# Attention, then a low-rank mixer, on one core: the low-rank sum laid out by transfers, mixing of one tile ahead of scores, conversions in other steps

## The chip, the cores and the metric

The kernel runs on one core of a Trainium2 chip. The metric is the device time of one launch in microseconds (us), as a median of several runs. One more execution was taken by the hardware profiler; all lines shown below come from it.

## The reference

Inputs are q, k, v of shape (4, 8, 768, 64) and eight decay factors lam in float32, and four weights U, V, w_ch1, w_ch2 in float64. Only what matters is shown:

```python
def _attn_ref(q, k, v, lam):            # block = 64
    for b in range(nb):
        intra = (qb @ kb^T) * Dmask          # lam ** (i - j), lower triangle
        intra = intra @ vb
        inter = (qb * lam_pow) @ kv_state
        out[:, :, sl] = intra + inter
        kv_state = lam_block * kv_state + (kb * rev_pow)^T @ vb

def _moe_ref(x, U, V, w_ch1, w_ch2):    # x: (4, 768, 512), all heads side by side
    xt = x.transpose(0, 2, 1)
    h = xt @ U @ V                       # U: 768 x 32, V: 32 x 768, over the sequence
    u = x + h.transpose(0, 2, 1)
    ch = np.maximum(u @ w_ch1, 0.0) @ w_ch2   # 512 x 2048 and 2048 x 512
    return u + ch
```

So each of the four batches needs all of its 768 rows of x before the low-rank sum (x^T U, 512 x 32) is known; then every row tile gets its share of V added (the "mixing"), and the result u goes into two large products.

## The kernel before

**Stages.** The rows of the four batches are cut into 24 tiles of 128 rows, six in a batch. Step s computes the attention of tile s and, on the side, finishes tile `done` = s - 7 of the batch before (mixing, transposing, splitting into parts for the product). After step 23 comes the first large product in "units": a unit (`hidden`) is one slice of 128 of the 2048 hidden columns for a pair of 512-row groups, with 24 matmuls of 128x512; into the first units the leftovers of the last batch are put (`rest`, L893 and on). Then comes the second product. The order of instructions on every engine is written out by hand in the list `pieces` (L653 to L685) and, for the first units, in `rest`, `at` and `side`: every engine runs its own instructions in that order and waits where an operand isn't there.

**One step (L659 to L685).** For tile s: `fade` (ScalarE, L401, from the third tile of a batch), `mix` and `turn` of earlier tiles (TensorE, L567 and L630), `split` (ScalarE L644, VectorE L645), `prep` of tile s+1 (transposes of q and k on TensorE, L361; copies out by ScalarE, L367; then the load of a later q tile), `scale` (GpSimd, L392 for q and L381 for k), `mixed` (VectorE, L579), `intra` and `state` (L455, L427), the next v load on ScalarE's queue, `inter` (L466, then ScalarE's copy of x, L472), `scores` of tile s+1 (L408), `low` at the end of a batch (L482), `aside` (a piece of weight conversion), `masked` of tile s+1 (VectorE, L417), then `store` of a finished tile and the next k load on SyncE's queue. At s = 0, 4, 5 and 6 `aside` comes after `masked`.

**The low-rank sum.** `low(b)` (L477) makes x^T U of batch b in one PSUM tile `pp` of 128 x 128: four groups of 32 partitions, one for each quarter of the 512 columns. It shares its PSUM slot (tag "px") with the output of `intra`. The mixing reads `p_hl`, four groups of 32 partitions by 512 columns: in each half of the partitions (two groups) the high part of 256 columns in the left half, the low part in the right half. Each quarter is needed on two groups of partitions, its own and a neighbour's. ScalarE copies two quarters of `pp` side by side into `p_f` (L492), VectorE the other two (L524) and then masks off the high bits into `p_h` (L527). In the next step three pieces follow by `next_of_low`: four ScalarE copies place the high part (L535), GpSimd subtracts twice for the low part (L539), two ScalarE copies place the low part on the other two groups (L546). The last batch goes another way (L499 to L520), which is not touched.

**The mixing.** `mix(s)` is four matmuls of 64 x 128 by 64 x 256 into the right half of the PSUM tile `pm` (one buffer); the transposes of the tile before (`turn(s - 1)`) write the left half of the same buffer. `mixed(s)` adds the result to x.

**Conversions.** The weights come as float64 words and are made into float32 by steps: fetches on SyncE's queue (L146), `one` (VectorE L166 and, unless `apart`, `mantissa` L155; ScalarE L173 and L174), `two` (L184), `three` (L192), `four` (L197), and for w_ch1 the split `five` (ScalarE L215), `six` (L220), `seven` (L227). `aside(s)` issues them; the ScalarE parts are held back to `late`. The numbers in L744 to L747 say in which step each is put; what is left at NS (24) goes into the first units (L907). The words go in turn into the buffers of `words_pool` (L139).

Of the kernel before, what the change touches and what calls it, by code (L numbers as in the profile page):

```python
# [8 lines left out]
FP32 = mybir.dt.float32  # L9
# [9 lines left out]
def kernel(  # L19
# [91 lines left out]
    def weight_steps(dst, src, n, rows=P, in_parts=False, apart=False):  # L111
# [23 lines left out]
        def fetch_part(i):  # L135
            if i == 0 and plain:
                st["loads"] = list(pieces(dst()))
            elif i == 0:
                words_pool.append(words_pool.pop(0))  # L139
                words = words_pool[-1].tile([P, 2 * C], U32, tag="words", name="words")  # L140
                words = words[0:rows, 0 : 2 * n]
                st["loads"] = list(pieces(words))
                st["w"] = words.rearrange("p (n two) -> p n two", two=2)
# [331 lines left out]
    pps, others = {}, {}  # L475

    def low(b):  # L477
# [12 lines left out]
        pps[b] = rows_f = tmp("p_f")[0:R]  # L490
        for g in range(2):
            nc.scalar.copy(rows_f[:, g * P : (g + 1) * P], pp[g * R : (g + 1) * R])  # L492
        others[b] = pp

    def low_rows(b):

        pp, t = pps.pop(b), tmp("p_h")[0:R]
        own = [(slice(g * R, (g + 1) * R), slice(g * P, (g + 1) * P)) for g in range(G)]
        if b == B - 1:  # L499
            h, h2, l, l2 = (p_hl[g * R : (g + 1) * R] for g in range(G))  # L500
# [21 lines left out]
        rows_f, pp = pp, others.pop(b)  # L522
        for g in range(2, G):
            nc.vector.tensor_copy(  # L524
                out=rows_f[:, g * P : (g + 1) * P], in_=pp[g * R : (g + 1) * R]
            )
        nc.vector.tensor_scalar(t.bitcast(U32), rows_f.bitcast(U32), HI, None, ALU.bitwise_and)  # L527
        wide = [slice(x * 2 * P, (x + 1) * 2 * P) for x in range(2)]

        def place(g, low):  # L530
            return p_hl[g * R : (g + 1) * R, wide[low]]

        def spread():
            for g in range(G):
                nc.scalar.copy(place(g, 0), t[:, wide[g // 2]])  # L535

        def low_part():
            for x in range(2):
                nc.gpsimd.tensor_tensor(  # L539
                    out=place(2 * x, 1), in0=rows_f[:, wide[x]], in1=t[:, wide[x]],  # L540
                    op=ALU.subtract,
                )

        def spread_low():
            for x in range(2):
                nc.scalar.copy(place(2 * x + 1, 1), place(2 * x, 1).bitcast(FP32))  # L546

        pps[b] = [spread, low_part, spread_low]
# [105 lines left out]
    for s in range(NS):  # L654
# [7 lines left out]
        step += [("mix", done)] * mixes + [("turn", done - 1)] * turns  # L662
# [3 lines left out]
        step += [("next_of_low", b - 1)] * rows + [("next_of_low", b - 1)] * rows  # L666
        step += [("scale", s + 1)] * more
        step += [("mixed", done)] * mixes
# [404 lines left out]
```

## Time and profile before

| | us |
|---|---|
| median of 3 runs | 653.47 (651.42 to 654.1) |
| profiled execution, its own time | 651.42 |
| its span, first to last instruction | 649.6 |
| steps of batch 0, to the scores of tile 6 | 0 to 31.18 |
| steps of batches 1, 2, 3 (to the scores of tile 12, of tile 18, to the first unit) | 31.18 to 58.27 to 86.99 to 115.36 |
| first four units with leftovers | 115.36 to 145.0 |
| the rest of both products | 145.0 to 649.6 |

TensorE's busy time in these five stretches is 28.62 of 31.18, 26.56 of 27.09, 27.29 of 28.72, 27.40 of 28.37, and 29.25 of 29.64 us; from 145 to 640 us it is 494.97 of 495. The granted clock is 1.000 throughout. Because matmuls are pipelined and their ends are modelled, a short stall can hide in TensorE's busy time; the distance from one step's scores to the next step's scores shows it better. In undisturbed steps (42.44 to 55.37 us) that distance is 4.31 to 4.32 us.

### The profile page before, as it was taken

The numbers are of one execution on the slowest core, as the hardware profiler recorded it, in microseconds if no ns is written. First come the engines' busy times: TensorE is split into PE (matmuls) and PEld (weight loads), VectorE is DVE, ScalarE is ACT, GpSimd is POOL, SyncE is SP. The second block draws the span as 40 slices with busy tenths as digits, with TensorE's granted clock in tenths as the row PEclk, the third lists the DMA queues.
The fourth block names the chain that finished last, engine by engine and source line by source line (L and its number), as shares of the span: only waits on it lengthen the run. The fifth ranks groups of instructions, "written<-read, shape, count | busy, mean of one in ns | idle before, by whom it ended". The sixth has DMA issues, their size and how long they took to land.

```text
span 649.6 us, 13396 instructions
## 1 busy us (share of the span) xinstructions
PE 639.9 (99%) x5242; PEld 538.1 (83%) x5242; DVE 441.2 (68%) x722; ACT 273.1 (42%) x506; POOL 116.4 (18%) x98
## 2 busy tenths in 40 slices
PE   8999999999999999999999999999999999999997
PEld 7889889788888888888888888888888888888886
DVE  6776879658997777777796254685575665755854
ACT  4676767435664444444454221332322322322320
POOL 4466868240000000000000000030030300300300
PEclk9999999999999999999999999999999999999999
DMA  9989994265876656566687999864363363453521
GB/s 229 247 200 251 231 252 124 77 216 167 290 256 227 211 210 211 210 211 211 210 292 267 321 324 399 285 216 147 97 227 98 115 211 97 160 164 98 178 82 65
DMA packets 131776, 131.29 MB, mean 202 GB/s; under 512 B 81346, under 2 KB 89794, under 8 KB 131714
## 3 DMA queue, kind: packets, MB, share of 16 engines
q1 hardware_dynamic: 106592, 124.02, 59.8%
q10 hardware_dynamic: 25122, 6.42, 4.4%
q8 instruction: 41, 0.67, 0.5%
q14 instruction: 21, 0.17, 0.1%
HBM read 80.09 MB, written 50.33 MB: 201 GB/s over the span
## 4 chain that ended last, share of the span: by engine, by line
PE 94%; ACT 2%; DVE 1%; DMA 1%; issue 1%; DVEq 0%; ACTq 0%
PE pz L837 26%; PE pz L971 13%; PE pz L969 13%; PE pd L973 13%; PE pd L848 13%; PE pss L408 3%; PE px L455 3%; PE px L466 2%; PE pqk L361 1%; PE pkv L427 1%; DMA qraw<-in_q_dram 1%; PE pp L482 1%; PE pm L567 1%; PE pm L630 1%; PE put L608 1%
## 5 line engine op out<-in xcount | busy, mean ns | idle before, releaser
L837 PE MATMUL pz<-u_hl,w 128*128 128x512 f32 x768 | 184.5, 390 | 0.0
L837 PEld LDWEIGHTS pz<-u_hl,w 128*128 128x128 f32 x768 | 143.6, 188 | 30.1 <-ACT r L844 0.3
L971 PE MATMUL pz<-w_hl,m 128*128 128x512 f32 x384 | 148.6, 389 | 0.0
L969 PE MATMUL pz<-w_hl,m 128*128 128x512 f32 x384 | 148.2, 389 | 0.0
L973 PE MATMUL pd<-w_d,m 128*128 128x512 f32 x384 | 147.4, 389 | 0.0
L952 ACT ACTIVATE m<-rm 128x512 fp32r<-128x512 f32 x96 | 60.6, 632 | 183.5 <-PE pd L973 123.0
L953 DVE SCALAR_TENSOR_TENSOR m<-rm,m 128x512 fp32r<-128x512 f32 x96 | 71.5, 747 | 96.0 <-ACT m L952 95.9
L998 POOL TENSOR_TENSOR o<-o,u 128x512 f32<-128x512 f32 x20 | 29.8, 1522 | 433.4 <-DVE o L994 433.4
L853 DVE SCALAR_TENSOR_TENSOR r<-pd,r 128x512 f32<-128x512 f32 x96 | 61.7, 685 | 60.1 <-ACT r L844 48.0
L848 PE MATMUL pd<-u_d,w 128*128 128x512 f32 x384 | 95.9, 390 | 0.0
L973 PEld LDWEIGHTS pd<-w_d,m 128*128 128x128 f32 x384 | 72.1, 188 | 15.3 <-DVE m L954 0.5
L971 PEld LDWEIGHTS pz<-w_hl,m 128*128 128x128 f32 x384 | 72.1, 188 | 15.0
L969 PEld LDWEIGHTS pz<-w_hl,m 128*128 128x128 f32 x384 | 72.1, 188 | 14.9
L848 PEld LDWEIGHTS pd<-u_d,w 128*128 128x128 f32 x384 | 71.8, 188 | 14.8
L844 ACT ACTIVATE r<-pz 128x512 f32<-128x512 f32 x96 | 51.8, 590 | 64.8 <-PE pz L837 64.8
L954 DVE SCALAR_TENSOR_TENSOR m<-m 128x512 fp32r<-128x512 f32 x96 | 74.7, 780 | 3.0
L417 DVE TENSOR_TENSOR sm<-pss,mask 128x512 f32<-128x512 f32 x48 | 30.9, 684 | 15.4 <-PE pss L408 15.2
L215 ACT ACTIVATE w<-wf 128x512 fp32r<-128x512 f32 x32 | 20.3, 634 | 35.7 <-DVE wf L197 27.4
L173 ACT ACTIVATE sc<-sc,ends 128x512 f32<-128x512 uint32 x30 | 21.6, 721 | 23.2 <-DVE sc L166 23.1
L455 PE MATMUL px<-vraw,sm 128*64 128x64 f32 x768 | 28.4, 225 | 2.7 <-ACT u_hl L644 0.9
L455 PEld LDWEIGHTS px<-vraw,sm 128*64 128x64 f32 x768 | 25.2, 137 | 4.7 <-issue 1.3
L408 PE MATMUL pss<-qt,kt 64*128 64x128 f32 x384 | 28.8, 290 | 0.1
(92 smaller groups left out, 619.4 us busy)
## 6 DMA issues: line engine op xcount, KB each, us to landing
r_d<-r SPq DMA_DIRECT2D x96, 256.0 KB, 2.6
rm<-r_d SPq DMA_DIRECT2D x96, 256.0 KB, 2.7
words<-in_moe_w_ch_dram SPq DMA_DIRECT2D x30, 512.0 KB, 4.4
w_d<-w SPq DMA_DIRECT2D x16, 768.0 KB, 3.4
w_hl<-w_d SPq DMA_DIRECT2D x16, 512.0 KB, 6.1
u_d<-x_nat SPq DMA_DIRECT2D x24, 256.0 KB, 4.0
u<-u_d SPq DMA_DIRECT2D x24, 256.0 KB, 4.2
qraw<-in_q_dram SPq DMA_DIRECT2D x23, 256.0 KB, 4.1
```

Of the source, the lines that this page charges most:

```text
L408: nc.tensor.matmul(out=pss[:, x, a, :], lhsT=kt[half[x], a, :], rhs=qt[half[x], a, :], start=True, stop=True,)
L455: nc.tensor.matmul(out=px[half[t], x, a, :], lhsT=sm[:, x, a, half[t]], rhs=vr[:, 2 * a + x, :], start=(a == 0), stop=(alone and a == HP - 1),
L837: nc.tensor.matmul(out=like(acc[g][0], g), lhsT=w[:, n, ct, :], rhs=columns(uhl[g][:, n], g, ct), start=(ct == 0 and n == 0), stop=(ct == ...
L844: nc.scalar.mul(rs[g], acc[g][0], 4096.0 + 1.0)
L848: nc.tensor.matmul(out=like(acc[g][1], g), lhsT=w[:, 2, ct, :], rhs=columns(ud[g], g, ct), start=(ct == 0), stop=(ct == CT - 1),)
L853: nc.vector.scalar_tensor_tensor(rs[g], acc[g][1], 4096.0, rs[g], ALU.mult, ALU.add)
L952: nc.scalar.activation(out=m[:, 0], in_=r, func=AF.Relu, scale=NEAR)
L953: nc.vector.scalar_tensor_tensor(m[:, 1], r, 0.0, hi, ALU.max, ALU.subtract)
L954: nc.vector.scalar_tensor_tensor(m[:, 2], hi, E, low, ALU.mult, ALU.subtract)
L969: nc.tensor.matmul(out=pz, lhsT=m[:, 0, cols], rhs=hl[:, 0], start=first, stop=False)
L971: nc.tensor.matmul(out=pz, lhsT=m[:, 1, cols], rhs=hl[:, 1], start=False, stop=end)
L973: nc.tensor.matmul(out=pd, lhsT=m[:, 2, cols], rhs=dd, start=first, stop=end)
```

## The change

Five things are altered. (1) For batches 0 to 2 the low-rank sum is copied out of PSUM by one ScalarE copy of 128 x 128; in the next step four ScalarE copies of 32 x 128 round it into its own places, four GpSimd subtractions of 32 x 128 make the low part, and four SBUF-to-SBUF transfers of 32 x 2 x 128 on SyncE's queue lay both parts into the neighbour's places. The VectorE work and the mask are gone. (2) For the second tile of a batch's steps (c == 1, where the first tile of the batch before is mixed) `mix` and `mixed` come just ahead of the next scores, after `inter`. (3) The conversions of w_ch1's first two slices sit in other steps; the second slice's `three`, `four`, `five`, `six` move to the end of unit 0 and `seven` to the end of unit 1. (4) U's fetch moves from before step 0 to step 1 and its conversion from steps 1 and 2 to steps 2 and 3; V's fetches move from step 0 to step 2. (5) `words_pool` is turned the other way round, so that the buffers are used in another order.

```diff
-                words_pool.append(words_pool.pop(0))
-                words = words_pool[-1].tile([P, 2 * C], U32, tag="words", name="words")
+                words_pool.insert(0, words_pool.pop())
+                words = words_pool[0].tile([P, 2 * C], U32, tag="words", name="words")
...
     def low(b):
...
-        pps[b] = rows_f = tmp("p_f")[0:R]
-        for g in range(2):
-            nc.scalar.copy(rows_f[:, g * P : (g + 1) * P], pp[g * R : (g + 1) * R])
-        others[b] = pp
+        pps[b] = tmp("p_f")[:, 0:P]
+        nc.scalar.copy(pps[b], pp)
...
     def low_rows(b):
...
-        rows_f, pp = pp, others.pop(b)
-        for g in range(2, G):
-            nc.vector.tensor_copy(
-                out=rows_f[:, g * P : (g + 1) * P], in_=pp[g * R : (g + 1) * R]
-            )
-        nc.vector.tensor_scalar(t.bitcast(U32), rows_f.bitcast(U32), HI, None, ALU.bitwise_and)
-        wide = [slice(x * 2 * P, (x + 1) * 2 * P) for x in range(2)]
-        def place(g, low):
-            return p_hl[g * R : (g + 1) * R, wide[low]]
-        def spread():
-            for g in range(G):
-                nc.scalar.copy(place(g, 0), t[:, wide[g // 2]])
-        def low_part():
-            for x in range(2):
-                nc.gpsimd.tensor_tensor(
-                    out=place(2 * x, 1), in0=rows_f[:, wide[x]], in1=t[:, wide[x]],
-                    op=ALU.subtract,
-                )
-        def spread_low():
-            for x in range(2):
-                nc.scalar.copy(place(2 * x + 1, 1), place(2 * x, 1).bitcast(FP32))
-        pps[b] = [spread, low_part, spread_low]
+        def place(g, of, low):
+            return p_hl[g * R : (g + 1) * R, low * 2 * P + (of % 2) * P :][:, 0:P]
+        def own():
+            for g in range(G):
+                rows, at = pp[g * R : (g + 1) * R], place(g, g, 0)
+                nc.scalar.copy(at, rows)
+                nc.gpsimd.tensor_tensor(
+                    out=place(g, g, 1), in0=rows, in1=at.bitcast(FP32), op=ALU.subtract
+                )
+        def other():
+            for g in range(G):
+                at, of = (
+                    p_hl[x * R : (x + 1) * R].rearrange("r (l h c) -> r l h c", l=2, h=2)
+                    for x in (g ^ 1, g)
+                )
+                nc.sync.dma_start(
+                    out=at[:, :, g % 2].bitcast(FP32), in_=of[:, :, g % 2].bitcast(FP32)
+                )
+        pps[b] = [own, other]
...
-        step += [("mix", done)] * mixes + [("turn", done - 1)] * turns
+        step += [("mix", done)] * (mixes and c != 1) + [("turn", done - 1)] * turns
...
-        step += [("next_of_low", b - 1)] * rows + [("next_of_low", b - 1)] * rows
+        step += [("next_of_low", b - 1)] * rows
         step += [("scale", s + 1)] * more
-        step += [("mixed", done)] * mixes
+        step += [("mixed", done)] * (mixes and c != 1)
...
-        step += [("next_of_low", b - 1)] * rows
         both = [("intra", s), ("state", s)]
         step += (both if s > NT else both[::-1]) + [("next_v", s), ("inter", s)]
+        step += [("next_of_low", b - 1)] * rows
...
+        step += [("mix", done), ("mixed", done)] * (mixes and c == 1)
         step += [("scores", s + 1)] * more
...
-        (u_side, (-1, 1, 1, 2, 2)),
-        (v_steps(), (0, 0, 3, 3, 4, 4, 4, 5, 5)),
-        (w1_steps(0, True), (8, 9, 10, 11, 13, 14, 15, 16, 16, 17, 19)),
-        (w1_steps(1, True, True), (15, 16, 17, 18, 20, 20, 21, 22, 23, 23, NS, NS)),
+        (u_side, (1, 2, 2, 3, 3)),
+        (v_steps(), (2, 2, 3, 3, 4, 4, 4, 5, 5)),
+        (w1_steps(0, True, True), (8, 9, 10, 11, 12, 14, 15, 16, 17, 17, 20, 21)),
+        (w1_steps(1, True, True), (15, 16, 17, 18, 18, 22, 23, NS, NS, NS, NS, NS)),
...
-    aside(-1)
...
-    side = list(zip((0, 0), last)) + list(zip((0, 3, 3, 3, 4, 4, 4, 4), w1_steps(2)))
+    side = list(zip((0, 0, 0, 0, 1), last)) + list(zip((0, 3, 3, 3, 4, 4, 4, 4), w1_steps(2)))
```

## The prediction

> **What bounds the kernel now.** First the page's head: TensorE is busy nearly all the time, and the chain that ended last is almost all TensorE.
>
> ```profile
> PE 639.9 (99%) x5242; PEld 538.1 (83%) x5242; DVE 441.2 (68%) x722; ACT 273.1 (42%) x506; POOL 116.4 (18%) x98
> ...
> PE 94%; ACT 2%; DVE 1%; DMA 1%; issue 1%; DVEq 0%; ACTq 0%
> ```
>
> The change takes no matmul away, so it can only win back stalls or add some. The stretch from 145 to 640 us has TensorE busy for 494.97 of 495: nothing to win there, and what moves there (the words buffers' new order) costs nothing while TensorE's inputs are ready as now; if a fetch there came late, one unit would wait. All that counts lies ahead of 145 us. There I read TensorE's timeline from one step's scores (L408) to the next; a full undisturbed step takes 4.31. These lines show the stalls:
>
> ```profile
> 11.95 0.47 PE L361 MATMUL pqk<-ident,qraw 64*128 64x64 f32 x8 [0.40 <-DMA qraw<-in_q_dram]
> 16.37 0.47 PE L361 MATMUL pqk<-ident,qraw 64*128 64x64 f32 x8 [0.44 <-DMA qraw<-in_q_dram]
> ...
> 64.20 1.16 PE L408 MATMUL pss<-qt,kt 64*128 64x128 f32 x16
> ...
> 69.25 1.16 PE L408 MATMUL pss<-qt,kt 64*128 64x128 f32 x16
> ...
> 72.26 1.24 PE L455 MATMUL px<-vraw,sm 128*64 128x64 f32 x32 [0.87 <-ACT qt L367]
> ...
> 125.80 0.66 PE L608 MATMUL put<-ident,x_nat 128*128 128x128 f32 x4 [0.39 <-DVE x_nat L575]
> ```
>
> The reader sees three kinds: q tiles late in batch 0; steps of 5.05 instead of 4.31 where a batch's first tile is mixed (64.20 to 69.25), and the step after it (5.33, to 74.58); and a wait for VectorE in the first units. Summed over the three batch changes the steps are about 6 us longer than the undisturbed ones (5.27, 5.05, 5.33, 5.31, 4.96 against 4.31, and some 1.6 in the three steps before): that bounds the gain.
>
> Third, VectorE's and ScalarE's timelines, by which each part is costed:
>
> ```profile
> 14.74 1.11 DVE L155 TENSOR_SCALAR m<-words 128x192 uint32<-128x192 uint32 x1
> ...
> 16.16 1.28 DVE L417 TENSOR_TENSOR sm<-pss,mask 128x512 f32<-128x512 f32 x2
> ...
> 20.66 1.28 DVE L417 TENSOR_TENSOR sm<-pss,mask 128x512 f32<-128x512 f32 x2
> ...
> 70.05 1.51 DVE L155 TENSOR_SCALAR m<-words 128x512 uint32<-128x512 uint32 x1
> ```
> ```profile
> 63.10 1.66 ACT L535 CAST vp<-p_h 32x256 fp32r<-32x256 f32 x4
> ...
> 64.78 0.83 ACT L546 CAST vp<-vp 32x256 fp32r<-32x256 f32 x2
> ...
> 67.36 0.59 ACT L367 COPY kt<-pqk 128x512 f32<-128x512 f32 x1
> ```
>
> Conversion pieces stand ahead of `masked` (L417) on VectorE, and the placing copies ahead of the k copy (L367) that TensorE's `state` waits for.
>
> **U's and V's words: +1.1 us.** SyncE issued U at 7.99, ahead of two q tiles that then came 0.40 and 0.44 late. Moved behind k3, q3, k4, q4 and q5, U frees q3 (the first late tile, q2, is ahead of it and stays late). But `one` of U now stands ahead of step 2's `masked`. When does U land? SyncE's issues from 8.9 on take 1.69, 1.84, 1.69 and again some 1.6, so U is issued at about 15.9 and lands 4.5 later (U's own landing before), 20.4; by bytes it is a little earlier, since V's 192 KB no longer go ahead of it: 19.6. I take 20.0. Then L166, L155, L184: 2.05 as measured from 14.11 to 16.16, or about 1.1 if each takes the 0.36 that L184 took there. `masked` starts at 21.1 to 22.1 instead of 20.66, TensorE's `intra` 0.81 later (20.66 to 21.50 before, rounded), at 21.9 to 22.9 against 21.50: +0.4 to +1.4, +0.8 taken. In step 3 `three` and `four` of U (1.53 at 19.13 to 20.66) now join V's 2.2 ahead of `masked`: TensorE has 3.8 of work until it needs that result, VectorE needs 2.0 (masked, kv) + 2.2 to 3.7, so 0 to 1.4 more, 0.3 taken, since GpSimd is idle then. Bounds for the whole 0 to +3.0: below nothing if U comes by 18.5.
>
> VectorE's L155 took 1.11 for 192 columns while GpSimd's L381 ran (14.66 to 15.73), yet 0.48 on average for 512 columns later, mostly beside an idle GpSimd. The Trainium skill ("SBUF — State Buffer", SBUF: two separate sides) calls this a lock: the one that starts second is blocked for the other's whole instruction. By it U's three pieces cost 1.1 where no GpSimd instruction is under way at 20 us (the next, L392, comes near 21), and the sum would be 0.4 lower than with the middle value.
>
> **Copied out once, laid by transfers, mixing later.** I work out batch 2 (steps 12 to 14). ScalarE: two copies of 0.26 become one, but u_hl waits for TensorE until 61.6 anyway: nothing. VectorE loses two copies and a mask (0.59 + 0.42): they weren't last there. Four copies of 128 columns cost about 0.30 each (0.403 at 256 columns, 0.618 at 512), 1.2 instead of 1.66 + 0.83. v's issue and x's copy follow, to 65.4 (before 66.23), then u_hl, q and k copies (0.6, 0.49, 0.59 as shown): the k copy ends at 67.1 instead of 67.95, and `state` and `inter` (0.62 each) end at 68.45. GpSimd: 0.806 at 256 columns and 1.006 at 384 give 0.6 at 128, four pieces from 63.5 to 65.95; L392, which `inter` needs, follows to 67.25: in time. If a piece took 0.8, it would be 68.05 and cost 0.4. The last transfer is issued at 66.05 and lands 2.2 later, 68.3. That 2.2 is the unknown: the smallest transfers of this trace (out, 128 KB) land in 1.8, q tiles in the half-empty queue at 34.22 in 3.0, medians of k, q, v, u_d 4.0 to 5.2; these are 32 KB and the queue ahead has only one q tile, so the low end is nearest; both ends are kept. The k load and the store behind them on SyncE start some 2 us later; the k tile issued near 67 then is used by GpSimd at 74.1 and takes some 5 to land: covered, by 2 us. `mix` (0.43) at 68.45, scores at 68.9 instead of 69.25: -0.35. `mixed` (0.68) is done while scores (1.09) run, so the next `mix` into the same buffer isn't held.
>
> The Trainium skill speaks against such transfers ("DMA: Bandwidth & Descriptors", Rules for kernel authors: under 64 KB one pays mostly overhead; Anatomy of one DMA gives about 2.0 us fixed). One fixed cost, as an estimate 2.1, changes nothing here; four that did not overlap would be 8.4, 6 us more at each batch.
>
> Step 14 then loses its 0.87 stall: L166 and L155 (69.51 to 71.47) held `masked`; now L166 sits in step 12 and L155 in step 14, so scores follow at 73.2 instead of 74.58. Batch 2 in all -1.3. Batch 1 by the same sums: the k copy gains 1.3, but GpSimd's four pieces start at 36.0 behind V's part, L392 ends at 39.8 and the transfers land at 40.8, scores 41.3 instead of 41.53: -0.2. Batch 3: ScalarE also gets L215 (0.63) there, the k copy gains 0.2, `mix` is now behind it: +0.25; but the stall of 104.94 (step 5 us instead of 4.31; L166 and L155 at 102.07 to 104.24 ahead of `masked`) goes: -0.65. Batch 3 -0.4. Sum -1.9; bounds, by landings of 1.8 or 4.5 and pieces of 0.45 or 0.8: -3.2 to +4.6.
>
> **Second slice's last conversions in unit 1: +1.2 us.** After unit 0's last r (126.94) VectorE now has L192 0.68, L197 0.69, waits for ScalarE's L215 0.63, then L220 0.74, with handovers 2.95, before L575 (0.68) ends at 130.55. TensorE needed that x at 129.28 (`put`), and nothing else is in its queue: +1.25. Before, only L220 and L227 stood there and L575 ended at 128.86. L227 now comes after unit 1 and is needed 3.6 us into unit 2: hidden. Bounds 0 to +1.6.
>
> **Sum.** +1.1 - 1.9 + 1.2 = +0.4, 650.0 of span. The profiled execution took 651.42, the lowest of the three; against the median 653.47 I predict 653.9. About 0.5%, 3.3 us, is what a measurement here can tell from no change. The likeliest case's own range is 650.5 to 656.5.
>
> **Rivals.** (1) Transfers land late: slower. If the four land like k, q and v tiles, 4.5 instead of 2.2, each first `mix` stalls 2.3 more (batch 3 has 0.4 of slack): 3 x 2.3 - 0.4 = +6.5, 660.4. For: those loads share the queue, and DMA is near full in these stretches. Against: 32 KB behind one q tile. It decides from a landing of 3.3 on (+2.8). (2) U's conversion is held at both places with GpSimd beside it: +3.0 instead of +1.1, and transfers 0.6 later: 653.9 + 1.9 + 1.4 = 657.2. (3) U lands by 18.5, unit 1 hides the conversions by running its pd part late, and the batch changes give -3.2: 653.47 - 3.2 - 0.4 = 649.9, faster. For: steps 13, 14 and 20 have 6 us to give; against: ScalarE still sets the k copy. That the transfers don't take the place of the copies can't be: the instruction order shows them.
>
> **Numbers.** Forecast 0.56, (1) 0.18, (2) 0.08, (3) 0.18. Faster by over 0.5% 0.18, within 0.5% 0.56, slower 0.26. The range reaches from (3) to (1): 649.5 to 660.5.
>
> **What would show it.** Right: VectorE's L166 on U waiting for a DMA near 18 to 20 us and `intra` of step 3 near 22.4; `state` of step 13 some 0.8 earlier after its scores; transfers landing in 2 to 2.5; no stall in step 14; `put` waiting about 1.2 in unit 1. Wrong: `pm` (L567) waiting over 1 us for DMA at a batch change; no wait on U's words; a step of 4.31 in unit 1's place, that is, no stall there.

## The result, and the profile after

| | before | after |
|---|---|---|
| median of 4 runs each, us | 653.31 (651.42 to 654.1) | 660.07 (659.43 to 660.93) |
| profiled execution, us (span) | 651.42 (649.6) | 659.43 (657.6) |
| mean granted clock over the span | 1.000 | 0.995 |

The ratio is 1.0109, interval 1.0084 to 1.0134: the change makes the kernel 1.1% slower, 6.8 us in the medians, 8.0 us in the spans. First the page of the kernel after: its first part and the shares of the chain that ended last.

```profile
PE 641.1 (97%) x5242; PEld 540.1 (82%) x5242; DVE 432.0 (66%) x713; ACT 268.6 (41%) x497; POOL 116.2 (18%) x104
...
PE 92%; DMA 2%; DVE 2%; ACT 2%; issue 1%; SPq 0%; ACTq 0%; POOL 0%; DVEq 0%
```

VectorE and ScalarE have less to do than before (432.0 and 268.6 us against 441.2 and 273.1), and the span grew all the same: TensorE is 97% busy instead of 99%, and its busy time itself is 1.2 us larger with the same 5242 matmuls. Stalls and slower matmuls are to be looked for. The starts of the scores (L408) of each tile say where; the last column is after minus before, and what counts is where it changes:

| scores of tile | before | after | difference |
|---|---|---|---|
| 6 (end of batch 0) | 31.18 | 32.20 | +1.02 |
| 9 (batch 1 changed) | 45.85 | 47.48 | +1.63 |
| 15 (batch 2 changed) | 74.58 | 74.68 | +0.10 |
| 18 | 86.99 | 87.94 | +0.95 |
| 19 | 92.66 | 93.60 | +0.94 |
| 20 | 97.97 | 105.27 | +7.30 |
| 23 | 111.58 | 118.31 | +6.73 |
| the `put` in unit 1 that waits | 129.28 | 137.04 | +7.76 |

The step from tile 19 to tile 20 alone gives 6.4 of the 8.0. TensorE's timeline of the kernel after has these lines (start, duration, what, and in brackets the idle time ahead of it and what ended it):

```profile
42.77 0.51 PE L562 MATMUL pm<-vp 64*128 64x256 f32 x3 [1.20 <-DMA vp<-vp]
...
72.44 1.15 PE L455 MATMUL px<-vraw,sm 128*64 128x64 f32 x32
...
87.66 0.34 PE L466 MATMUL px<-kv,qs 64*64 64x64 f32 x7 [0.57 <-issue]
...
95.09 0.41 PE L361 MATMUL pqk<-ident,kraw 64*128 64x64 f32 x8
100.85 1.98 PE L455 MATMUL px<-vraw,sm 128*64 128x64 f32 x32 [5.35 <-issue]
102.58 1.10 PE L427 MATMUL pkv<-vraw,ks 128*64 128x64 f32 x16
103.61 1.13 PE L466 MATMUL px<-kv,qs 64*64 64x64 f32 x32
104.68 0.80 PE L562 MATMUL pm<-vp 64*128 64x256 f32 x4
...
137.04 0.66 PE L603 MATMUL put<-ident,x_nat 128*128 128x128 f32 x4 [0.88 <-DVE x_nat L570]
```

In the order of the lines: the first mix of batch 1 waits for a transfer; the stall of step 14 is gone (72.26 had 0.87 before); a short stop in step 17; then 5.35 us of idleness in step 19, and after it matmuls that take far longer than elsewhere (px 1.98 instead of 1.15, px of L466 1.13 instead of 0.69); at the end the `put` of unit 1. "issue" means that the profile shows no releaser, so the wait is followed through VectorE's timeline:

```profile
20.23 0.26 DVE L166 TENSOR_SCALAR sc<-words 128x192 uint32<-128x192 uint32 x1 [2.70 <-DMA words<-in_moe_U_dram]
...
24.70 0.35 DVE L166 TENSOR_SCALAR sc<-words 64x384 uint32<-64x384 uint32 x1 [1.46 <-DMA words<-in_moe_V_dram]
...
99.72 0.43 DVE L166 TENSOR_SCALAR sc<-words 128x512 uint32<-128x512 uint32 x1 [5.59 <-DMA words<-in_moe_w_ch_dram]
100.07 1.28 DVE L417 TENSOR_TENSOR sm<-pss,mask 128x512 f32<-128x512 f32 x2
```

`masked` (L417), which TensorE's px needs, stands behind a conversion (L166) that waited 5.59 us for its words. SyncE's queue says why the words were late:

```profile
91.50 0.38 SPq L282 DMA_DIRECT2D qraw<-in_q_dram  x1
93.61 3.63 SPq L539 DMA_DIRECT2D vp<-vp  x4
97.29 0.58 SPq L146 DMA_DIRECT2D words<-in_moe_w_ch_dram  x1
```

The last part of the second slice's words is fetched at 97.29 only. The table of the change has `one` of that slice in step 18, the step of its own last fetch, and the four transfers of batch 3 stand ahead of that fetch on SyncE: they wait for GpSimd's pieces and take 3.63 us to issue. The third thing is the clock. The windows of the kernel after give, for each stretch, its length and each engine's busy time with its instructions, then the granted clock (third from the end):

```profile
97.00:98.00 1.00, 0.00 (x0) 0.00 (x0) 0.00 (x0) 0.00 (x0) 1.00 (x2) 1.00 0.19 46
99.00:100.00 1.00, 0.00 (x0) 0.00 (x0) 0.28 (x1) 0.00 (x0) 0.00 (x0) 0.50 0.90 318
101.00:102.00 1.00, 1.00 (x22) 1.00 (x24) 0.94 (x2) 0.67 (x1) 0.00 (x0) 0.50 1.14 257
104.00:105.00 1.00, 1.00 (x30) 0.88 (x28) 0.58 (x4) 0.19 (x1) 1.00 (x2) 0.50 0.10 23
105.00:106.00 1.00, 1.00 (x14) 1.00 (x14) 0.49 (x1) 1.00 (x4) 1.00 (x1) 0.67 1.00 227
```

Before the wait the clock is 1.00, during it it falls to 0.50 and stays there until about 105.7, almost five microseconds after work has come back. That is why one wait of 5.35 us makes a step 6.4 us longer.

### The profile page after: what moved, and what is told of

Read it like the earlier page. It is cut to its first block, busy times and chain, and to the rows that moved or that the text cites. A ratio compares the mean times of both kernels' runs of the same rounds, so it can differ in the third digit from the quotient of the medians.

```text
span 657.6 us, 13405 instructions
## 1 busy us (share of the span) xinstructions
PE 641.1 (97%) x5242; PEld 540.1 (82%) x5242; DVE 432.0 (66%) x713; ACT 268.6 (41%) x497; POOL 116.2 (18%) x104
## 4 chain that ended last, share of the span: by engine, by line
PE 92%; DMA 2%; DVE 2%; ACT 2%; issue 1%; SPq 0%; ACTq 0%; POOL 0%; DVEq 0%
PE pz L832 26%; PE pd L843 13%; PE pz L964 13%; PE pz L966 13%; PE pd L968 13%; PE px L455 4%; PE pss L408 3%; PE px L466 2%; PE pqk L361 2%; PE pkv L427 1%; DMA rm<-r_d 1%; PE pm L562 1%; PE pp L482 1%; DMA words<-in_moe_V_dram 1%; PE pm L625 1%
## 5 line engine op out<-in xcount | busy, mean ns | idle before, releaser
L417 DVE TENSOR_TENSOR sm<-pss,mask 128x512 f32<-128x512 f32 x48 | 30.9, 685 | 19.4 <-PE pss L408 19.4
L215 ACT ACTIVATE w<-wf 128x512 fp32r<-128x512 f32 x32 | 20.3, 634 | 38.6 <-DVE wf L197 30.7
L408 PE MATMUL pss<-qt,kt 64*128 64x128 f32 x384 | 28.8, 290 | 0.0
```

The source lines that it names most:

```text
L408: nc.tensor.matmul(out=pss[:, x, a, :], lhsT=kt[half[x], a, :], rhs=qt[half[x], a, :], start=True, stop=True,)
```

## The experiments

All times are ratios to the kernel before on the same chip, with 95% intervals. Single executions scatter: the kernel before itself gave 650.6 to 656.1 us. What a part does is therefore read from the steps of the profiled execution, and what it is worth from the ratio. Steps scatter too, in batch 1 most of all. From tile 6 to tile 9 the same program took 0.5 us less than the kernel before in e4, but 2.7 and 3.4 us more in e8 and e10; and four runs that share another program there (after, e1, e2, e7) took 0.6, -0.1, 1.25 and 2.8 us more. And e3, which is the kernel before up to step 17, is 3.7 us behind it at tile 6, by one stop of TensorE of 1.87 us and the lowered clock behind it. So what one execution shows of batch 1 is not a price.

| run | what | ratio | interval |
|---|---|---|---|
| after | the change | 1.0109 | 1.0084 to 1.0134 |
| e1_one20 | second slice's `one` in step 20 | 1.0042 | 1.0018 to 1.0065 |
| e2_fetch14 | its fetches one step earlier | 1.0035 | 1.0005 to 1.0065 |
| e3_before_one18 | before, with `one` in step 18 | 1.0016 | 0.9987 to 1.0046 |
| e4_old_uv | U and V as before | 1.0072 | 1.0055 to 1.0089 |
| e5_lay_only | laying and mixing alone | 1.0036 | 1.0020 to 1.0051 |
| e6_copies | e1 with copies for transfers | 1.0056 | 1.0035 to 1.0077 |
| e7_unit_back | second slice's table as before | 1.0063 | 1.0041 to 1.0085 |
| e8_best | e4, fetches from 14, `one` in 19, all but two pieces of the second slice before the units | 1.0018 | 0.9999 to 1.0037 |
| e9_mix_behind | e4, fetches from 14, `one` in 18, first mix behind the scores | 1.0085 | 1.0057 to 1.0112 |
| e10_mix_ahead | the same, first mix ahead of the scores | 1.0017 | 0.9995 to 1.0039 |
| e11_pool_queue | transfers on GpSimd's queue | 1.0208 | 1.0181 to 1.0236 |
| e12_tables_only | before, with only the slices' tables moved | 0.9995 | 0.9981 to 1.0009 |

**Is it the late words? (e1, e2).** Two ways to have the words in time, each one line of the table in the kernel after:

```diff
-(w1_steps(1, True, True), (15, 16, 17, 18, 18, 22, 23, NS, NS, NS, NS, NS)),
+(w1_steps(1, True, True), (15, 16, 17, 18, 20, 22, 23, NS, NS, NS, NS, NS)),   e1
+(w1_steps(1, True, True), (14, 15, 16, 17, 18, 22, 23, NS, NS, NS, NS, NS)),   e2
```

> Only the step in which VectorE first reads the second slice's words is moved: from step 18 to step 20, nothing else. Theory (the words' last part is issued by SyncE behind the four transfers of batch 3 and VectorE's L166 waits for it with the mask product queued behind it): the step from 93.60 to 105.27 us shrinks from 11.67 to about 5.3 us, L166 no longer waits for a DMA, the granted TensorE clock stays at 1.00 from 95 to 106 us, and the time is 660.1 - 6.4 = about 653.7 us. Rival A (the transfers themselves or their landing hold the step): TensorE still waits 3 us or more in that step, 657 us or more. Rival B (part of the wait only moves, to the mix product that waits for the transfers): a step of 6.3 to 7.0 us, 654.5 to 655.5 us.

> The reading stays in step 18, but each of the four word fetches of the second slice is asked for one step earlier (14 to 17 instead of 15 to 18), so that the last one is on SyncE's queue before the four transfers of batch 3. Theory (late words): as with the later reading, about 653.7 us, no wait of L166 for a DMA in step 18. Rival (VectorE's two conversion pieces in front of the mask product in step 18 are the cost, not the words): 658 us or more, the step stays above 9 us.

TensorE's timeline of e1 in the same step:

```profile
92.67 1.16 PE L408 MATMUL pss<-qt,kt 64*128 64x128 f32 x16
...
94.68 1.24 PE L455 MATMUL px<-vraw,sm 128*64 128x64 f32 x32
...
97.04 0.50 PE L562 MATMUL pm<-vp 64*128 64x256 f32 x4
97.38 0.83 PE L408 MATMUL pss<-qt,kt 64*128 64x128 f32 x12
```

The step takes 4.71 us (92.67 to 97.38) in e1 and the same 4.71 in e2 (98.31 to 103.02), instead of 11.67, with the transfers still there; no L166 waits for these words, and the clock is 1.00 from 92 to 109 us in the profiled execution of e1. The two agree although in e2 VectorE's piece stays in step 18: it is the words, not the piece and not the transfers' landing. Of the 6.96 us, 5.35 are the idleness; the other 1.6 are what the lowered clock adds. In the ratios e1 and e2 win 0.0067 and 0.0074 of the 0.0109, 4.4 to 4.8 us rather than 6.4: e1 expected 653.7 us against 653.3, that is 1.0006, and got 1.0042. Part of the difference is that a stall comes back (e1's step of tile 21, 101.75 to 107.36, takes 5.61 us, 4.32 in the kernel after: px waits 1.2 us, and `masked` stands behind L220 and L166 on VectorE); the rest is in the parts below. The profiled execution of e2 lies 4.1 us above e2's median: it loses 3.5 us in steps 17 and 18, by a stop of TensorE that is taken up further down.

**Is the early reading enough? (e3).** The kernel before with 18 in place of the first 20:

```diff
-(w1_steps(1, True, True), (15, 16, 17, 18, 20, 20, 21, 22, 23, 23, NS, NS)),
+(w1_steps(1, True, True), (15, 16, 17, 18, 18, 20, 21, 22, 23, 23, NS, NS)),
```

> The kernel before, with the second slice's first reading in step 18 instead of 20 (its mantissa piece stays at 20), the low-rank sum still laid by copies. The words' last fetch was issued there at 90.99 us and such fetches took 5.0 to 6.1 us to land, so the words are there at 96.0 to 97.1; VectorE was free for L166 at about 93.2 and the mask product started at 93.87. Theory (the early reading and the transfers ahead of the fetch on SyncE make the loss together, each has its share): TensorE's px of step 19 moves from 95.45 to about 97.7, that is 2.3 us slower than before, 655.6 us (bounds 654.3 to 656.5), with the granted clock hardly touched. Rival A (the early reading alone makes the whole loss): 659 us or more. Rival B (without the transfers the early reading is free): 653.0 to 653.8 us.

VectorE's timeline of e3:

```profile
100.21 0.43 DVE L166 TENSOR_SCALAR sc<-words 128x512 uint32<-128x512 uint32 x1 [2.84 <-DMA words<-in_moe_w_ch_dram]
```

The step takes 6.76 us instead of 5.31, +1.45, of which 0.65 come back in step 21 (4.31 instead of 4.96). So the early reading waits even without transfers, half as long, and costs 0.8 us net by these steps: more than B and far less than A, if the steps are believed; the ratio alone can't tell it from no change. The fetch was issued 1.67 us ahead of the scores of tile 19 here, and 3.69 us behind them in the kernel after. TensorE's wait in the step was 1.63 us, and the clock stayed at 1.00.

**Is it SyncE's queue or the DMA engines? (e11).**

```diff
-                nc.sync.dma_start(
+                nc.gpsimd.dma_start(
                     out=at[:, :, g % 2].bitcast(FP32), in_=of[:, :, g % 2].bitcast(FP32)
                 )
```

> The changed kernel with only the queue of the four transfers changed: GpSimd issues them instead of SyncE. Theory (it is SyncE's queue that delays the words in step 18, not the transfers on the DMA engines): the words' last fetch is issued about 94 us instead of 97.29, L166 waits 2 to 3.5 us instead of 5.6, the step of 11.67 us takes 6.5 to 8.5; GpSimd's four issues stand in front of qs and cost up to 1 us at each batch change; ratio 1.003 to 1.008. Rival (the DMA engines are the cause): the words land at 99 us or later all the same and the step stays at 10.5 us or more, ratio 1.010 or more.

The words' fetch is issued 1.67 us ahead of the scores of tile 19 again, and L166 waits 2.27 us instead of 5.59: the words come as in e3. That is SyncE's queue, as the theory said. GpSimd issues the transfers of batch 3 only at 106.72, though, when the words have been read (105.43), so e11 doesn't show what transfers under way do to words. The kernel after does: there the fetch was issued at 97.29, behind the transfers, and L166 started at 99.72, 2.4 us later; in e3, without any transfer, it took 5.0 us (95.17 to 100.21). Once issued, the words were not slow. What the theory had wrong is the price at the other end. GpSimd's timeline and TensorE's in batch 1:

```profile
41.91 2.29 POOL L539 DMA_DIRECT2D vp<-vp  x4
```
```profile
44.84 1.43 PE L562 MATMUL pm<-vp 64*128 64x256 f32 x4 [3.02 <-DMA vp<-vp]
```

The issues stand in GpSimd's program behind its work for q and k (L392, L381, to 41.9) and start at 41.91, 4.4 us after the scores of tile 7 (37.49); in the kernel after SyncE's first issue came 0.6 us after them (37.49 and 36.93). The first mix then waits 3.0, 3.3 and 2.4 us in the three batch changes, and the clock falls behind each of them; the step in question is 9.67 us long, above the 6.5 to 8.5 expected, since 2.42 us of it are such a wait.

**What do U's and V's words cost? (e4).**

```diff
-        (u_side, (1, 2, 2, 3, 3)),
-        (v_steps(), (2, 2, 3, 3, 4, 4, 4, 5, 5)),
+        (u_side, (-1, 1, 1, 2, 2)),
+        (v_steps(), (0, 0, 3, 3, 4, 4, 4, 5, 5)),
...
         load_next(name)
+    aside(-1)
     load_next("k")
```

> The changed kernel with U's and V's words asked for and converted in the steps of the kernel before. Theory (asking later cost 1.0 us up to the scores of tile 6, by VectorE's L166 waiting 2.7 us on U and 1.5 on V ahead of the mask product): scores of tile 6 start at about 31.2 instead of 32.20 us, the q tiles wait 0.4 us each again, the rest of the run keeps its 11.67-us step, and the time is about 659.0 us. Rival (the later words pay for themselves further on, by freeing loads in batch 1): the gain of 1.0 is lost again by tile 9 and the time is 660.0 us or more.

Scores of tile 6 start at 31.24 instead of 32.20: 0.96 us, as expected. The q tiles waited only 0.2 us in that time and the k tiles 0.5. The difference to the kernel before is -0.41 us at tile 9, so in this execution nothing is lost again in batch 1 (there TensorE waited 0.3 us for vp, 1.2 in the kernel after; e8 and e10, the same up to there, waited 1.75 and 1.76), and -1.18 at tile 15. The step of tile 19 stays at 11.24 us. The ratio falls by 0.0037, 2.4 us, more than the 1.0 expected.

**What are laying and mixing worth alone? (e5, e12).** e5 is the change with U's and V's lines as in e4, the slices' lines of the kernel before and the old order of the words' buffers; e12 is the kernel before with only the two slices' tables moved (the second slice with early fetches). From the kernel after to e5, then from the kernel before to e12:

```diff
-(w1_steps(0, True, True), (8, 9, 10, 11, 12, 14, 15, 16, 17, 17, 20, 21)),
-(w1_steps(1, True, True), (15, 16, 17, 18, 18, 22, 23, NS, NS, NS, NS, NS)),
+(w1_steps(0, True), (8, 9, 10, 11, 13, 14, 15, 16, 16, 17, 19)),
+(w1_steps(1, True, True), (15, 16, 17, 18, 20, 20, 21, 22, 23, 23, NS, NS)),
```
```diff
-(w1_steps(0, True), (8, 9, 10, 11, 13, 14, 15, 16, 16, 17, 19)),
-(w1_steps(1, True, True), (15, 16, 17, 18, 20, 20, 21, 22, 23, 23, NS, NS)),
+(w1_steps(0, True, True), (8, 9, 10, 11, 12, 14, 15, 16, 17, 17, 20, 21)),
+(w1_steps(1, True, True), (14, 15, 16, 17, 18, 22, 23, 23, 23, 23, NS, NS)),
```

> The changed kernel with all four tables of conversions (U, V, both slices of w_ch1) and the order of the words' buffers put back: what is left of the change is the single copy, the four transfers and the later mixing. Theory (these are worth next to nothing, because the k copy of ScalarE sets the step either way; the 1.5 us won in batch 2 came from the conversions put elsewhere): step 14 keeps its wait of 0.9 us ahead of px, the batch changes give -0.5 to +0.5 us together, ratio 0.999 to 1.001. Rival A (laying and mixing won the 1.5 us): scores of tile 15 come 1.0 us or more earlier against those of tile 12, ratio 0.997. Rival B (the transfers themselves cost, by a wait of mix for DMA at one or more batch changes): a wait of 0.5 us or more for vp, ratio 1.002 or more.

> The kernel before (low-rank sum laid by copies, mixing at the start of the step, U's and V's words as there) with only the conversions of the two slices of w_ch1 moved: the first slice as in the changed kernel, the second asked for in steps 14 to 17, read in step 18, its pieces up to the fourth done in step 23. Theory (what the change won in batches 2 and 3 came from these tables, and what it lost in batch 1 from the laying): the waits of 0.87 us in step 14 and of 0.5 us in step 21 go, no wait for words in step 18, no wait for vp in batch 1; the steps of tiles 12 to 15 together 0.9 us shorter, those of 20 to 23 0.6 us, about 1.5 us in all, 0.9975 (0.996 to 0.9995). Rival A (the copies of the low-rank sum and the pieces moved meet on VectorE or ScalarE at the batch change): no gain, 0.9995 to 1.002. Rival B (reading in step 18 costs also with early words): a step above 5.8 us there, more than 1.002.

TensorE's timeline of e5:

```profile
43.59 0.50 PE L562 MATMUL pm<-vp 64*128 64x256 f32 x3 [1.66 <-DMA vp<-vp]
...
75.54 1.19 PE L455 MATMUL px<-vraw,sm 128*64 128x64 f32 x32 [1.37 <-DVE sm L417]
```

The first line is a new wait for a transfer, the second the old stall of step 14, which stays and grows (0.87 before). From tile 7 to tile 9 e5 takes 11.01 us, the kernel before 9.59: +1.4; from 12 to 14 it takes 10.74 against 10.98: -0.2, and the next step gives that back (5.85 against 5.33), so that batch 2 is 0.3 us longer at tile 15. Laying and mixing alone win nothing in the end, since VectorE's L166 and L155 still hold `masked` in step 14; the ratio is 1.0036: rival B of its expectation. In e12, steps 12 to 14 together are 1.0 us shorter (58.20 to 73.51 against 58.27 to 74.58; tile 14 to 15 takes 4.32 instead of 5.33) and there are no transfers that a mix could wait for: 1.0 of the 1.5 us that the change won in batch 2 is the tables' work. But e12's step of tile 19 grows from 5.31 to 5.98 us, because ScalarE now has L215 between the copies of the low-rank sum, and mix waits for the last of them:

```profile
92.45 0.63 ACT L215 ACTIVATE w<-wf 128x512 fp32r<-128x512 f32 x1
93.10 0.83 ACT L546 CAST vp<-vp 32x256 fp32r<-32x256 f32 x2
```

That is rival A in one batch: the profile shows 1.06 us won up to tile 23 instead of 1.5, and the ratio (0.9995) can't be told from no change.

**What do the transfers buy against copies? (e6).** e1 with four ScalarE copies in the transfers' place:

```diff
-                nc.sync.dma_start(
-                    out=at[:, :, g % 2].bitcast(FP32), in_=of[:, :, g % 2].bitcast(FP32)
-                )
+                nc.scalar.copy(at[:, :, g % 2], of[:, :, g % 2].bitcast(FP32))
```

> The kernel of the later reading (second slice's first conversion in step 20) with the four transfers replaced by four ScalarE copies of the same 32 x 256 values at the same place in the program. Theory (transfers cost nothing on the path once the words are out of their way, and buy ScalarE's time): four copies of about 0.4 us, 1.6 us, stand in front of u_hl, q and k copies at each batch change, TensorE waits for the k copy, 0.5 to 1.2 us at each, so 1.5 to 3.6 us slower than with the transfers, ratio to the kernel before 1.006 to 1.010. Rival (transfers land late or hold SyncE): copies are equal or faster, ratio 1.004 or less, and the mix product of batch 1 comes earlier.

ScalarE's timeline of e6 in batch 2, and TensorE's:

```profile
67.03 1.69 ACT L539 CAST vp<-vp 32x256 fp32r<-32x256 f32 x4
68.74 0.60 ACT L637 ACTIVATE u_hl<-pm 128x512 fp32r<-128x512 f32 x1
69.24 0.58 ACT L367 COPY qt<-pqk 128x512 f32<-128x512 f32 x1
69.70 0.60 ACT L367 COPY kt<-pqk 128x512 f32<-128x512 f32 x1
```
```profile
70.41 0.69 PE L427 MATMUL pkv<-vraw,ks 128*64 128x64 f32 x16 [1.35 <-POOL ks L381]
```

The profile puts the wait down to GpSimd's L381, but that had ended at 69.89; what ends at 70.30, just ahead, is the k copy, and pkv is written there into the PSUM slot that q and k are copied out of. So the wait is the k copy's, as the theory had it, and longer than its 0.5 to 1.2 us: 1.35 here, 1.25 and 1.71 in the other two batches; the step of tile 13 takes 6.18 us against 5.23 in e1. In the ratio it is 0.0014 above e1, less than the intervals can tell, and just below what was expected (1.006 to 1.010); in batch 1 (tile 7 to 9) it takes 10.44 us, between e1 with transfers that came in time (9.39) and e5 with late ones (11.01).

**Unit 1 (e7).** The kernel after with the second slice's table as before:

```diff
-(w1_steps(1, True, True), (15, 16, 17, 18, 18, 22, 23, NS, NS, NS, NS, NS)),
+(w1_steps(1, True, True), (15, 16, 17, 18, 20, 20, 21, 22, 23, 23, NS, NS)),
```

> The changed kernel with the second slice's conversions at the steps of the kernel before (first reading in step 20, all but two pieces done before the units). Theory (conversions in unit 1 hold x of the first put there): put of unit 1 comes 3.5 us behind the one ahead of it, as before, instead of 4.5 us; the 11.67-us step is gone too; TensorE waits about 0.5 us in step 21 again; so 660.1 - 6.4 - 1.2 + 0.5 = 653.0 us, ratio 0.999 to 1.001. Rival (the wait in unit 1 is not the conversions' but that of GpSimd's or ScalarE's other work): put stays at 4.5 us, ratio 1.002 to 1.004.

The `put` comes 3.48 us after the one ahead of it (131.21 to 134.69), as in the kernel before, and 4.51 in the kernel after: the stall in unit 1 is the conversions'. The time was missed. VectorE's timeline of e7 ahead of tile 22:

```profile
104.08 1.52 DVE L220 TENSOR_TENSOR w<-wf,w 128x512 fp32r<-128x512 f32 x1
105.52 1.28 DVE L166 TENSOR_SCALAR sc<-words 128x512 uint32<-128x512 uint32 x1
106.72 1.48 DVE L155 TENSOR_SCALAR m<-words 128x512 uint32<-128x512 uint32 x1
108.13 1.28 DVE L417 TENSOR_TENSOR sm<-pss,mask 128x512 f32<-128x512 f32 x2
```

The change had put the first slice's L220 into step 20, and e7 put L166 and L155 back there too: 4.1 us in front of `masked`, TensorE idle for 2.46, and the step of tile 21 7.90 us long, behind it a lowered clock. So the first slice's table can only move if the second's moves with it. Batch 1 lost 2.8 us besides in this execution (a wait of 1.84 us for vp, and the lowered clock behind it).

**All mended (e8), and the first mix behind the scores (e9, e10).** All three have U and V of e4; the second slice's line is the first below in e8 and the second in e9 and e10, and e9 also turns the order round:

```diff
-(w1_steps(1, True, True), (15, 16, 17, 18, 18, 22, 23, NS, NS, NS, NS, NS)),
+(w1_steps(1, True, True), (14, 15, 16, 17, 19, 20, 21, 22, 23, 23, NS, NS)),   e8
+(w1_steps(1, True, True), (14, 15, 16, 17, 18, 22, 23, 23, 23, 23, NS, NS)),   e9, e10
...
-        step += [("mix", done), ("mixed", done)] * (mixes and c == 1)
         step += [("scores", s + 1)] * more
+        step += [("mix", done)] * (mixes and c == 1)
...
         step += [("masked", s + 1)] * more
+        step += [("mixed", done)] * (mixes and c == 1)
```

> The changed kernel with U's and V's words as before, the second slice's words asked for in steps 14 to 17, read in step 19 and converted before the units. Theory (all three losses taken away, the gain of 1.2 to 1.5 us in batches 1 and 2 kept): 651 us, 1.5 to 2 us below the kernel before, ratio 0.997 (0.995 to 0.999). Rival A (a reading in step 19 stands in front of a mask product that has no slack): TensorE waits 0.5 us or more in steps 19 to 21 and the ratio is 0.999 to 1.002. Rival B (losses come back elsewhere because loads collide): more than 1.002.

> The changed kernel with U's and V's words as before, the second slice's words asked for in steps 14 to 17 and read in step 18 as there, its pieces up to the fourth done in step 23, and the first mix of each batch put behind the next scores instead of ahead of them. Theory (the first mix of batch 1 waits up to 1.8 us for the last of the four transfers, scores of 1.1 us behind it in TensorE's queue; with the order turned round the scores cover it): no wait for vp above 0.7 us, scores of tile 9 no later than in the kernel before, batches 2 and 3 won as in the runs before (1.0 us each), put of unit 1 after 3.5 us; about 650 us, ratio 0.997 (0.995 to 0.998). Rival A (scores put first only shift the wait behind them): a wait of 1.0 us or more stays, ratio as of the run beside it. Rival B (the pieces in step 23 or the mixed x hold something else): a new wait of 0.5 us or more after 90 us, ratio 0.998 to 1.001.

> The same kernel with the first mix ahead of the scores, as in the changed kernel. Theory: the mix of batch 1 waits 1.2 to 1.8 us for vp, with 1 us more where the granted clock falls behind it, and the ratio is 0.002 to 0.004 above that of the run beside it, 0.999 to 1.001. Rival (the wait comes only in some executions and costs nothing on the median): same ratio as the run beside it, within 0.001.

e8 reaches 1.0018 and does not beat the kernel before. In its profile the steps of batch 0 are the old ones (-0.12 at tile 6), batch 2 wins 1.6 (tiles 12 to 15), `put` comes after 3.48 us; but batch 1 loses 2.8 us: TensorE's timeline and windows there,

```profile
42.38 0.50 PE L562 MATMUL pm<-vp 64*128 64x256 f32 x3 [1.75 <-DMA vp<-vp]
```
```profile
43.00:44.00 1.00, 1.00 (x14) 1.00 (x14) 0.61 (x1) 0.00 (x0) 0.00 (x0) 0.51 0.99 224
44.00:45.00 1.00, 1.00 (x19) 1.00 (x17) 0.61 (x2) 0.00 (x0) 0.00 (x0) 0.50 0.67 193
```

The wait of 1.75 us is followed by half the clock, and the step of tile 8 takes 5.80 us instead of 4.32. e10 shows the same (1.76 us, then 5.94 us) and the same ratio, 1.0017. Batch 1 is not all that e8 loses: from tile 17 to 18 it loses 0.9 us by a stop of TensorE, and from tile 20 to 23 1.1 us, where px waits 0.91 us (at 107.31) with L220 and L155 together ahead of `masked`; that is rival A's wait, with another piece than the one that it named. e9, which was to hide the wait in batch 1, has the worst ratio of the three, 1.0085, where e10 was expected to lie above it. TensorE's timeline in batch 2:

```profile
76.30 0.47 PE L562 MATMUL pm<-vp 64*128 64x256 f32 x3 [1.51 <-DMA vp<-vp]
77.55 0.51 PE L562 MATMUL pm<-vp 64*128 64x256 f32 x4 [0.78 <-DVE x_nat L574]
78.73 1.95 PE L455 MATMUL px<-vraw,sm 128*64 128x64 f32 x32
```

The scores didn't cover the transfers (1.51 left), and the next tile's mix now stood directly behind and had to wait until VectorE, which had `masked` first, had emptied the one buffer `pm` (0.78); then px ran at half the clock. Scores put first only moved the wait and added one, and in batch 3 the second mix waited 1.75 us in the same way (at 108.22), again with the clock falling behind it: the waits of rivals A and B together, at a ratio that neither had expected.

## Why the prediction was right and where it was wrong

The forecast was no change, 653.9 us; the time came out at 660.07, 6.8 us slower than before, inside the range but outside the likeliest case's own (650.5 to 656.5). That it lies inside is luck: the range reached 660.5 only through rival 1, transfers that land late at all three changes, and most of the loss came from the words of w_ch1, which no rival named.

- **U's and V's words, +1.1.** Right in size, +1.02 at tile 6, and by mechanism: U's L166 waited 2.70 us for DMA and started at 20.23, where 20.0 had been taken. Two errors cancelled in that: U was issued at 14.98, not 15.9, and took 5.2 us to be read, not 4.1. The shares are others: U moved px from 21.50 to 21.80, +0.3 instead of +0.8, because L166, L155 and L184 took 0.26, 0.25 and 0.36 with GpSimd idle up to 20.90, so that `masked` started 0.74 after L166; the prediction had 1.1 for the three pieces where no GpSimd instruction is under way, and 2.05 otherwise. V's words, which no term spoke of as late, held the next px for 0.84. Six profiles with U and V late are 0.7 to 1.6 us behind at tile 6, five with U and V as before (e4, e5, e8, e10, e12) -0.3 to +1.1; e3 and e9 have a stop of TensorE of 1.87 and 2.05 us ahead of it.
- **Batch 1, -0.2.** Wrong: from tile 6 to tile 9 +0.6 after, and -0.5 to +3.4 in the seven others that lay by transfers on SyncE with mix ahead of the scores (e1, e2, e4, e5, e7, e8, e10). The mis-sized term is the landing of the last transfer. With the 1.02 us of tile 6 taken off, GpSimd's pieces started at 36.0 as predicted and took 2.0 us instead of 2.45; four issues took 0.69 each (2.78 in all), so that the last came at 39.70, 0.66 after the last piece, where 0.1 had been taken; these two nearly cancel. But mix went on at 42.77, 3.1 us after the last issue, where 2.2 had been taken. Rival 1's mechanism is real in batch 1, though not at all three changes, and its 660.4 us agrees with the result only by chance. Four transfers that don't overlap, 8.4 us in the prediction, did not occur: from the first issue at 37.49 to the mix it was 5.3 us.
- **Batch 2, -1.3.** Right: -1.53 from tile 9 to tile 15, and -1.0 to -1.6 from tile 12 to 15 in six more profiles of the same program there (e1, e2, e4, e7, e8, e10). The tables alone give 1.0 of it (e12); the other 0.5, predicted as 0.35 by the earlier k copy, comes with the laying only where the tables have moved too, as e5 shows.
- **Batch 3, -0.4.** This is the step that failed. It named what stands on SyncE behind the four transfers, "the k load and the store", and left out the fetch of words between them, though the table of the change puts `one` of the second slice into the step of its last fetch. So the tables' words were costed as in time. e1, e2, e3 and e11 show in its place: words read in the step of their last fetch (+1.45 in e3), with transfers ahead of that fetch on SyncE (the rest of 6.4), and a clock that halves in the wait (1.6 of it). The gain of 0.65 in step 21 came as predicted (-0.57 from tile 20 to 23).
- **Unit 1, +1.2.** Right: +1.0, and e7 takes it away.
- **Behind unit 1, nothing.** Right: from that `put` to the end the kernel before takes 520.3 us and the kernel after 520.6, with the words' buffers in their new order. What that order does ahead of it was not tried alone.
- Rivals 2 and 3 did not occur: GpSimd was idle beside U's conversion, and U landed near 20.2, not by 18.5.

The 0.85 us of step 17 are a stop in the middle of `inter` (25 matmuls, then 7), with no releaser in the profile. It is at the same two counts in e2 (1.67 us), e8 (0.66) and e10 (0.18), and not in e1 or before. The traces show what these four have in common: in all of them 4,289 instructions of TensorE lie ahead of the stop, and the other unexplained stops (e9's 2.05 us behind 705, e3's 1.87 behind 961, one of 0.51 in e5 behind 3,009) lie whole multiples of 256 from there. The page of the kernel after names a queue of the DMA that brings instructions:

```profile
q8 instruction: 41, 0.67, 0.4%
```

These are its packets, the MB that they moved and their share of the time; each packet has 16,384 bytes. 41 of them go with TensorE's 10,599 instructions, one for about 256. In the seven stops TensorE went on 1.2 to 1.5 us after such a packet had ended (in the kernel after at 87.66, the packet at 86.38). And in none of the fourteen profiles does TensorE pass such a place, 193 and n times 256 instructions from its start, earlier than 1.20 us after the end of the n-th packet. So the stops are waits for the next block of instructions, as far as the traces can show it; no run was made to test it, and why the block comes late in some executions is open. It is also open why the last transfer of batch 1 needs 2.1 us in e4 and 3.6 in e8, the same program there, with the same issue times on SyncE; it is inferred from when mix goes on, since the trace gives that transfer no landing of its own.

## What to carry to other kernels

When transfers are added to a queue, list everything issued behind them in that step, fetches above all, and look up who reads each one first: the issue of a transfer that waits for its data holds all that follows on that queue (here the fetch, to 97.29). A first reader in the step of its own last fetch has no slack, and everything behind it on its engine (here the mask product) inherits the wait. Give a TensorE stall of 1.5 us or more the slower clock behind it in the upper bound, as it may or may not come. And test a bundle of moved pieces part by part and in pairs: here the largest loss belonged to neither the laying nor the tables alone, but to the transfers of one ahead of a fetch of the other.

## What the runs showed of the hardware that was not expected

**Short stalls can halve the clock.** Waits of TensorE of 1.75 (e8, and e9 in batch 3), 1.76 (e10), 1.84 (e7) and 1.87 us (e3, batch 0) were followed by 3.4 us at 0.50 (worked out from the windows: 0.98 + 2 + 0.44 us in e8), which made the step 1.3 to 1.5 us longer in e7, e8 and e10; one of 1.51 with another of 0.78 behind it lowered it too (e9). After the 5.35 us it was 6.8 us, twice as much, and the same after 3.02 us in e11, but 3.4 after its 3.31. Waits of 1.20 (after), 1.63 (e3) and 1.66 us (e5) left the clock at 1.00; two of 1.67 did either (e2); and so did longer ones, 1.71 in e6 and these two, the first of e11, the second of e9:

```profile
106.56 1.24 PE L455 MATMUL px<-vraw,sm 128*64 128x64 f32 x32 [2.02 <-ACT kt L367]
22.28 0.49 PE L408 MATMUL pss<-qt,kt 64*128 64x128 f32 x4 [2.05 <-issue]
```

The windows of e5 after its wait of 1.66 us (mix went on at 43.59), to be set beside those of e8:

```profile
44.00:45.00 1.00, 1.00 (x19) 0.92 (x19) 0.69 (x1) 0.00 (x0) 0.00 (x1) 1.00 0.96 216
45.00:46.00 1.00, 1.00 (x28) 0.99 (x28) 0.98 (x2) 0.33 (x1) 0.00 (x0) 1.00 0.88 236
```

So between 1.5 and 2.1 us the length of a wait does not decide alone whether some 1.4 us come on top; what else does was not tried. The Trainium skill ("TensorE: Matmul & The Clock Gate", Part 1: The HAM clock gate) says that the clock is judged over a window of about 3.4 us that runs freely, and that one idle window brings half rate. The 3.4 and 6.8 us at 0.50 agree with its length, and where a wait falls in a window that runs freely may be what differs, which no run here shows; but the runs show half rate after 1.75 us of idleness, about half such a window, so here the measurement decides.

**Small transfers cost as much to issue as large ones.** Each SBUF-to-SBUF transfer of 32 KB took SyncE 0.585 us to issue at least, a load of 256 KB 0.37 to 0.43 in 14 of its 29 rows from 30 to 115 us and up to 1.47 in the others; where the trace gives the landing of the transfers, it was 1.8 to 3.7 us, median 2.3 (kernel after). Issued by GpSimd, they took 0.53 us at least and landed in 1.7 to 3.6, median 2.4 (e11).

**TensorE can stop for its own instructions.** The stops above, of 0.18 to 2.05 us, all lie a multiple of 256 instructions apart, and e3 lost 3.7 us by one of them.
